# Residual of one row tile through TensorE, its normalise read from PSUM, its rows sent by halves of columns

## The chip, the cores and the metric

The kernel runs on one core of a Trainium2 chip. The metric is the device time of one execution in microseconds (us); the median of several runs is quoted, with its lowest and highest. A profile records one execution; its clock starts at the first instruction, and its span is about 1.8 us shorter than the device time.

## The reference, cut to what matters

```
def _layernorm(x): return (x - mean(x)) / sqrt(var(x) + 1e-5)      # over the 1024 columns

x = A_x                                     # 1 x 2048 x 1024, bf16
x = x + A(_layernorm(x), A_w_r, A_w_i)      # 2-D real FFT, times a complex filter, inverse FFT
x = x + B(_layernorm(x), w1, b1, w2)        # MLP: 1024 -> 3584, mish (the activation), 3584 -> 1024
x = x + A(_layernorm(x), ...)               # the second spectral layer
x = x + B(_layernorm(x), ...)
```

The change touches the seam between the second and the third of these lines: the end of the first MLP, and the layer norm and data movement that open the second spectral layer.

## The kernel before

The 2048 rows lie in SBUF, the working memory on the chip, as 16 tiles of 128 rows (`XS[:, j, :]`, bf16). PSUM is the memory that takes the matmul results, here as fp32 in banks of 512 columns. TensorE makes the second product of the MLP per row tile `j` and column half `h`, 28 matmuls into one PSUM bank. VectorE then adds that bank to the rows and takes statistics:

```
def mm2(c, t, h):
    j = 4 * c + t
    ...
    self.group(fns, reads=ra + r_w2, writes=[self.r_bank[bank]])        # 28 matmuls
    xs = self.XS[:, j, h * 512:(h + 1) * 512]
    self.op(dve, lambda e: e.tensor_tensor(xs, PS[:, bank, :], xs, ALU.add),
            reads=[self.r_bank[bank]], writes=[self.r_xs[j]])
    if not last:
        self.stats_half(j, h)                                          # bn_stats of 512 columns
    if h == 0:
        return
    ...
            self.root(j, 1)             # j >= 14: sqrt on ScalarE, reciprocal on VectorE
        b = self.apply(j, out=True)     # (x - mean) * r, 128 x 1024, SBUF to SBUF
        if j == 15:
            self.xr_direct(j, b)
        else:
            self.xn_store(j, b)         # the other tiles go by way of HBM
```

Dependences are kept in records: `self.r_xs[j]` is one record for the whole 1024-column row tile. An operation that reads a record waits for its last writer. `group` puts all waits of a group ahead of its first matmul. The last tile's rows go straight from SBUF to the spectral layer's input, in 16 transfers of 16 KB dealt to three issuing engines in turn; the first spectral matmul needs the first eight (the upper 64 rows):

```
def xr_direct(self, j, b):
    for i in range(16):
        half, h = i // 8, i % 8
        n = slice(64 * half, 64 * half + 64)
        prog = (self.sp, self.act, self.pool)[i % 3]
        self.dma(prog, self.XR.ap[row_of(j, h):row_of(j, h) + 1, n, :], b.ap[n, h * P:(h + 1) * P], ...,
                 reads=[b.res], parts=[self.r_xr[2 * half]])
```

After the MLP, 24 filler matmuls (`spin`) keep TensorE busy until the data arrives.

## Time and profile before

| | before |
|---|---|
| device time, median of 3 (lowest to highest) | 1017.54 us (1015.78 to 1019.77) |
| profiled span, granted clock | 1016.2 us, 0.998 |
| start of the last tile's first-half add, to first spectral matmul ("the seam") | 514.70 to 527.71, 13.01 us |
| of that, from the last MLP matmul to the first spectral one | 6.99 us |

I measure the seam from the first-half add because its start is set by work ahead of the edit (the first-half matmuls), so the seam holds the whole effect of the edit and nothing else. Its chain is shown in the prediction below. Beside it stand two lines of TensorE's timeline of the kernel before (start us, us, engine, line, operation, count, and in brackets the idle ahead with what ended it):

```profile
520.54 5.34 PE L628 MATMUL PS<-FD,BD 128*128 128x512 bf16 x24
527.71 6.85 PE L611 MATMUL PS<-M,ARENA 128*128 128x128 bf16 x104 [1.83 <-DMA ARENA<-ARENA]
```

The filler covers 5.34 us, then TensorE idles 1.83 us until the transfers have landed. So from the last MLP matmul on TensorE is not what the seam waits for. Ahead of that point it is: a matmul added there costs its own 0.22 us, little beside the add of 0.72 us that falls away, if it can start at once.

### The profile page before, as it was taken

How to read it: one execution, taken by the hardware profiler on the slowest of the kernel's cores; microseconds unless marked ns; L12 is line 12 of the kernel's file. 1: busy time of each engine (PE TensorE's matmuls, PEld its weight loads, DVE VectorE, ACT ScalarE, POOL GpSimd, SP SyncE). 2: the span in 40 equal slices, each digit the busy share in tenths (PEclk: the TensorE clock that was granted, in tenths of full speed). 3: DMA queues.
4: the chain of work that ended last, by engine and by line, in shares of the span. 5: the costliest groups of instructions: out<-in, count | busy, mean ns of one | idle time of the engine just before them, and what ended most of it. 6: DMA issues, size and time to landing. Idle time of an engine off the chain costs nothing.

```text
span 1016.2 us, 13732 instructions
## 1 busy us (share of the span) xinstructions
PE 955.1 (94%) x5779; PEld 507.3 (50%) x5865; DVE 326.5 (32%) x679; ACT 347.3 (34%) x482; POOL 81.5 (8%) x114
## 2 busy tenths in 40 slices
PE   0799799999999999999999978999999999999998
PEld 0577575444444444444456757644444444444443
DVE  6797469002444000033347736830011100000111
ACT  7798384330000433300029847543100024330000
POOL 4651000000000000002511100000000000000000
PEclk9999999999999999999999999999999999999999
DMA  9979813562111220002932875246411212100000
GB/s 283 247 221 320 212 61 114 181 205 72 47 46 32 73 83 21 1 21 82 195 66 82 233 188 140 89 156 207 126 27 46 73 52 80 45 1 11 21 26 27
DMA packets 154205, 107.00 MB, mean 105 GB/s; under 512 B 74448, under 2 KB 133664, under 8 KB 154144
## 3 DMA queue, kind: packets, MB, share of 16 engines
q1 hardware_dynamic: 143056, 78.61, 27.3%
q0 software_dynamic: 8912, 25.84, 8.8%
q10 hardware_dynamic: 2176, 1.66, 0.5%
q8 instruction: 47, 0.77, 0.3%
q14 instruction: 14, 0.11, 0.0%
HBM read 80.85 MB, written 20.71 MB: 100 GB/s over the span
## 4 chain that ended last, share of the span: by engine, by line
PE 86%; DVE 4%; DMA 4%; ACT 4%; issue 1%; SPq 0%; POOL 0%; ACTq 0%; DVEq 0%; POOLq 0%
PE PS L1057 38%; PE PS L1040 37%; PE PS L771 2%; PE PS L697 2%; PE PS L792 2%; DMA ARENA<-c_bt 1%; PE PS L950 1%; ACT ARENA L441 1%; DMA ARENA<-u_scratch 1%; DVE ARENA L619 1%; DMA XS<-in_A_x_dram 1%; ACT ARENA L550 1%; PE PS L1006 1%; DVE ARENA L592 1%; PE PS L810 1%
## 5 line engine op out<-in xcount | busy, mean ns | idle before, releaser
L1040 PE MATMUL PS<-ARENA 128*128 128x512 bf16 (+1 forms) x1950 | 389.3, 358 | 2.5 <-DVE ARENA L1011 0.6
L1057 PE MATMUL PS<-ARENA 128*128 128x512 bf16 x1756 | 385.5, 379 | 1.9
L1044 ACT ACTIVATE ARENA<-PS,B 128x512 bf16<-128x512 f32 (+1 forms) x248 | 158.9, 645 | 410.9 <-PE PS L1040 410.6
L1040 PEld LDWEIGHTS PS<-ARENA 128*128 128x128 bf16 x1984 | 192.8, 98 | 193.8 <-DVE ARENA L1011 1.5
L1057 PEld LDWEIGHTS PS<-ARENA 128*128 128x128 bf16 x1792 | 175.4, 98 | 211.4
L1062 DVE TENSOR_TENSOR XS<-PS,XS 128x512 bf16<-128x512 f32 x64 | 44.2, 691 | 587.1 <-PE PS L1057 587.1
L460 DVE BATCH_NORM_STATS2 BN<-XS 128x6 f32<-128x512 bf16 x100 | 64.7, 675 | 6.2 <-DMA XS<-in_A_x_dram 5.0
L550 ACT ACTIVATE ARENA<-PS 128x1440 bf16<-128x1440 f32 (+3 forms) x26 | 28.0, 1095 | 28.0 <-DVE XS L972 24.4
L249 POOL DMA_DIRECT2D xn_scratch<-ARENA x12 | 6.5, 541 | 374.5 <-DVE ARENA L512 374.5
L771 PE MATMUL PS<-ARENA 128*128 128x256 bf16 x256 | 32.4, 273 | 4.1 <-DVE ARENA L760 3.2
L778 ACT ACTIVATE ARENA<-PS 128x1024 bf16<-128x1024 f32 x32 | 33.0, 1051 | 7.1 <-PE PS L771 7.1
L432 ACT ACTIVATE RS<-MV,EPS 128x2 f32<-128x2 f32 (+2 forms) x5 | 1.5, 298 | 96.8 <-DVE MV L463 96.2
L697 PE MATMUL PS<-FD,ARENA 128*128 128x256 bf16 (+1 forms) x256 | 31.8, 271 | 2.4 <-ACT ARENA L617 1.2
L749 ACT ACTIVATE ARENA<-PS 128x1024 bf16<-128x1024 f32 x32 | 32.5, 1044 | 4.5 <-PE PS L745 4.5
L771 PEld LDWEIGHTS PS<-ARENA 128*128 128x128 bf16 x256 | 24.2, 98 | 11.8 <-DVE ARENA L760 5.5
L753 DVE TENSOR_TENSOR ARENA<-ARENA 128x1024 bf16<-128x1024 bf16 x32 | 22.0, 688 | 20.4 <-ACT ARENA L749 20.3
L697 PEld LDWEIGHTS PS<-FD,ARENA 128*128 128x128 bf16 x256 | 24.4, 98 | 6.5 <-DVE ARENA L619 1.4
L820 ACT ACTIVATE ARENA<-PS 128x1024 bf16<-128x1024 f32 x26 | 26.7, 1063 | 2.4 <-PE PS L792 2.4
L792 PE MATMUL PS<-ARENA,BD 128*128 128x256 bf16 x192 | 24.9, 273 | 2.3 <-ACT ARENA L778 2.3
L950 PE MATMUL PS<-MT,ARENA 128*128 128x32 bf16 (+1 forms) x512 | 20.9, 195 | 4.5 <-DMA ARENA<-u_scratch 2.5
L512 DVE TENSOR_SCALAR ARENA<-XS,MV,RS 128x1024 bf16<-128x1024 bf16 x48 | 24.8, 542 | 1.0
L732 ACT ACTIVATE ARENA<-PS 128x1024 bf16<-128x1024 f32 x22 | 22.9, 1058 | 3.1 <-PE PS L697 3.1
(76 smaller groups left out, 515.5 us busy)
## 6 DMA issues: line engine op xcount, KB each, us to landing
ARENA<-in_B_w_dram SPq DMA_DIRECT2D x56, 512.0 KB, 3.9
ARENA<-in_B_w_dram SPq DMA_DIRECT2D x56, 256.0 KB, 4.1
u_scratch<-ARENA SPq DMA_DIRECT2D x14, 512.0 KB, 3.7
ARENA<-u_scratch SPq DMA_DIRECT2D x14, 512.0 KB, 6.1
w_scratch<-ARENA POOLq DMA_DIRECT2D x8, 512.0 KB, 6.2
ARENA<-w_scratch POOLq DMA_DIRECT2D x8, 512.0 KB, 5.4
out_dram<-XS SPq DMA_DIRECT2D x16, 256.0 KB, 2.0
ARENA<-xn_scratch POOLq DMA_DIRECT2D x15, 256.0 KB, 10.0
```

The source lines that it names most:

```text
L460: self.op(self.dve, lambda e: e.bn_stats(self.BN[:, j, 6 * h:6 * h + 6], self.XS[:, j, 512 * h:512 * h + 512]), reads=[self.r_xs[j]], part ...
L550: fn = (lambda e: e.activation(dst, src, ACT.Copy)) if scale is None else \
L697: fns.append(lambda e: e.matmul(dst, at(r), FD[:, t:t + n], start=start, stop=stop))
L749: self.op(act, lambda e: e.activation(x.ap.rearrange("p a b -> p (a b)"), ps, ACT.Copy, scale=SIG), reads=banks, writes=[x.res])
L771: fns.append(lambda e, c=c, part=part: e.matmul(ps[:, c * 256:(c + 1) * 256], yk.ap[:, part, c * P:(c + 1) * P], t[:, (128, 0)[part]:(384, ...
L778: self.op(act, lambda e: e.activation(v.ap[:, :, i, :], src, ACT.Copy), reads=banks, parts=[v.res])
L792: fns.append(lambda e, dst=dst, part=part, c=c: e.matmul(dst, BD[:, c:c + P], mov(kd, part), start=(part == 0), stop=(part == 1)))
L950: fns.append(lambda e, l=l: e.matmul(self.PS[:, bank + l // k, l % k * w:(l % k + 1) * w], self.UT.ap[:, u0 + l, :], self.MT[:, 8 * lo:8 * ...
L1040: fns.append(lambda e, db=db, bank=bank, fl=fl: e.matmul(PS[:, bank, 0:w], wb.ap[:, db, fl * P:(fl + 1) * P], x.ap[:, db, tok], start=(db ...
L1044: self.op(act, lambda e, bank=bank, ft=ft: e.activation(at.ap[:, ft, tok], PS[:, bank, 0:w], ACT.Mish, bias=self.B1[:, ft:ft + 1]), reads= ...
L1057: fns.append(lambda e, i=i, ft=ft: e.matmul(PS[:, bank, :], at.ap[:, ft, t * P:(t + 1) * P], W2[ft].ap[:, h * 512:(h + 1) * 512], start=(i ...
L1062: self.op(dve, lambda e: e.tensor_tensor(xs, PS[:, bank, :], xs, ALU.add), reads=[self.r_bank[bank]], writes=[self.r_xs[j]])
```

## The change

The intent is to shorten the serial chain at the seam. For the last tile's right half, the residual becomes an identity matmul at the head of the accumulation group, so the add on VectorE falls away. Statistics and normalise read PSUM directly. The normalise is split by columns, so that the left half of the rows leaves early. ScalarE writes the finished right half back to `XS` afterwards. The core of the diff:

```
-    def xr_direct(self, j, b):
-        b.unread = False
-        for i in range(16):
+    def xr_direct(self, j, b, rows):
+        for i in rows:
 ...
+    def finish_last(self, bank):
+        j, dve, ps = 15, self.dve, self.PS[:, bank, :]
+        rb, r = self.r_bank[bank], self.r_mv[15]
+        self.op(dve, lambda e: e.bn_stats(self.BN[:, j, 6:12], ps), reads=[rb], parts=[r])
+        self.op(dve, lambda e: e.bn_aggr(self.MV[:, j, :], self.BN[:, j, :]), reads=[r], writes=[r])
+        self.root(j, 1)
+        b = self.xn_out[0]
 ...
+        for h in range(2):
+            src = ps if h else self.XS[:, j, 0:512]
+            self.op(dve, lambda e, h=h, src=src: e.tensor_scalar(b.ap[:, 512 * h:512 * h + 512], src, mean, rs, ...),
+                    reads=[rb if h else self.r_xs[j], r, self.r_rs[j]], parts=[b.res])
+            self.xr_direct(j, b, range(4, 16) if h else range(4))
+        self.copy(self.act, self.XS[:, j, 512:1024], ps, [], [rb, self.r_xs[j]])
 ...   in mm2:
+            summed = not last and (j, h) == (15, 1)
+            if summed:
+                fns.append(lambda e: e.matmul(PS[:, bank, :], self.IDENT[:], self.XS[:, j, 512:1024], start=True, stop=False))
 ...
-            self.group(fns, reads=ra + r_w2, writes=[self.r_bank[bank]])
+            self.group(fns, reads=ra + r_w2 + ([self.r_xs[j], self.r_ident] if summed else []), writes=[self.r_bank[bank]])
+            if summed:
+                self.finish_last(bank)
+                return
```

More of the change, by code (lines that the diff above doesn't have):

```diff
@@ L541, in xr_direct @@
                      reads=[b.res], parts=[self.r_xr[2 * half]])
+    def finish_last(self, bank):
[5 more added lines that the diff above has]
+        b = self.xn_out[0]
+        assert not b.unread
+        mean, rs = self.MV[:, j, 0:1], self.RS[:, 2, j:j + 1]
+        b.res.begin()
+        for h in range(2):
+            src = ps if h else self.XS[:, j, 0:512]
+            self.op(dve, lambda e, h=h, src=src: e.tensor_scalar(b.ap[:, 512 * h:512 * h + 512], src, mean, rs, op0=ALU.subtract, op1=ALU.mult),
+                    reads=[rb if h else self.r_xs[j], r, self.r_rs[j]], parts=[b.res])
+            self.xr_direct(j, b, range(4, 16) if h else range(4))
+        self.copy(self.act, self.XS[:, j, 512:1024], ps, [], [rb, self.r_xs[j]])
     def pair(self):
@@ L1058, in mm2 @@
                     PS[:, bank, :], at.ap[:, ft, t * P:(t + 1) * P], W2[ft].ap[:, h * 512:(h + 1) * 512],
-                    start=(i == 0), stop=(i == NF - 1)))
-            self.group(fns, reads=ra + r_w2, writes=[self.r_bank[bank]])
+                    start=(i == 0 and not summed), stop=(i == NF - 1)))
+            self.group(fns, reads=ra + r_w2 + ([self.r_xs[j], self.r_ident] if summed else []), writes=[self.r_bank[bank]])
+            if summed:
+                self.finish_last(bank)
+                return
             xs = self.XS[:, j, h * 512:(h + 1) * 512]
@@ L1074, in mm2 @@
                     self.root(j, 1)
-                b = self.apply(j, out=True)
-                if j == 15:
-                    self.xr_direct(j, b)
-                else:
-                    self.xn_store(j, b)
+                self.xn_store(j, self.apply(j, out=True))
         w2v = self.w2.rearrange("(ft fp) d -> fp ft d", fp=P)
```

## The prediction

> **What bounds the kernel now.** I read the page first, for its shares and for the chain that ended last.
>
> ```profile
> span 1016.2 us, 13732 instructions
> PE 955.1 (94%) x5779; PEld 507.3 (50%) x5865; DVE 326.5 (32%) x679; ACT 347.3 (34%) x482; POOL 81.5 (8%) x114
> PE 86%; DVE 4%; DMA 4%; ACT 4%; issue 1%; SPq 0%; POOL 0%; ACTq 0%; DVEq 0%; POOLq 0%
> ```
>
> TensorE carries 86% of the chain, nearly all of it the two groups of MLP matmuls, which the change leaves alone but for one added matmul. Everything else that is edited runs once, at the seam between the first MLP and the second spectral layer, for the last of 16 row tiles. So the second view is the chain of waits restricted to that seam (columns: start us, us, what).
>
> ```profile
> 517.74 2.98 PE PS L1057 x13
> 520.72 0.03 issue
> ...
> 520.81 0.70 DVE XS L1062
> 521.52 0.02 issue
> 521.54 0.71 DVE BN L460
> 522.25 0.02 issue
> 522.27 0.22 DVE MV L463
> 522.49 0.03 issue
> 522.51 0.30 ACT RS L432
> 522.81 0.02 issue
> 522.84 0.17 DVE RS L434
> 523.01 0.03 issue
> 523.04 0.56 DVE ARENA L512
> 523.60 0.02 issue
> 523.62 0.57 ACTq L249
> 524.19 0.03 issue
> 524.22 0.86 ACTq L249
> 525.09 0.03 issue
> 525.12 2.25 DMA ARENA<-ARENA
> 527.37 0.35 issue
> 527.71 0.62 PE PS L611 x8
> ```
>
> The reader is to see a strictly serial stretch of 6.99 us, from the last MLP matmul (520.72) to the first spectral matmul (527.71): add of the residual, statistics, aggregate, root, reciprocal, normalise, then two transfer issues on ScalarE's queue ahead of a third that takes 2.25 us to land. That third is transfer 7 of 16 (ScalarE issues 1, 4, 7, ...); the first spectral group waits for transfers 0 to 7, the upper 64 rows. TensorE meanwhile runs 24 filler matmuls. The whole 6.99 us is 0.69% of the span: even if it vanished, the 2% line would not be crossed.
>
> The third view is the timeline of VectorE ahead of the seam, since the new matmul reads what VectorE writes there.
>
> ```profile
> 514.70 0.69 DVE L1062 TENSOR_TENSOR XS<-PS,XS 128x512 bf16<-128x512 f32 x1 [3.21 <-PE PS L1057]
> 515.43 0.69 DVE L460 BATCH_NORM_STATS2 BN<-XS 128x6 f32<-128x512 bf16 x1
> ```
>
> The first-half add starts only after the first-half matmuls are complete (514.70), and TensorE meanwhile goes straight on with the second half. I will need that below.
>
> **What the Trainium skill says.** "VectorE: DVE Perf Modes", section "The perf-mode tier table (the rule you actually need)": a tensor_scalar on bf16 in SBUF may run at 4x, any PSUM operand is capped lower, and its next section gives 1x for fp32 in PSUM. The trace agrees as far as it goes: the 128x1024 bf16 normalise took 547 ns, but a 128x1024 cast out of fp32 PSUM took 1214 ns. "TensorE: Matmul & The Clock Gate", "Back-to-back issue gap": about N/2.4+2.5 ns, 216 ns for 512 columns; here 36 matmuls in 7.77 us, 216 ns each. Same page, "Single matmul latency": (398+N)/2.4 ns, 379 ns, and the filler records do say 379 ns; so a restarted stream pays 379-216 = 163 ns once. "DMA: Bandwidth & Descriptors", "Anatomy of one DMA": about 2 us fixed whatever the size; the 16 KB pieces land 2.0 to 2.5 us after issue, so making work ready earlier can save only the issue ahead of that, not the landing.
>
> **The change part by part.** Times are on the clock of the profile above.
>
> (1) Residual through TensorE. The add of 0.70+0.02 = 0.72 us leaves the path. In comes an identity matmul of 216 ns at the head of the second-half group. It is not free to start at once: it reads the last tile's rows, and the kernel keeps one dependence record for the whole 1024-column tile, whose last writer is the first-half add. So TensorE, in order, must stop until 514.70+0.69 = 515.39, say 515.45 with semaphore and weight load. Without the change the second-half group starts at about 520.70-0.38-27x0.216 = 514.49. The stall is 515.45-514.49 = 0.96 us. The columns it needs (512 to 1023) were long ready, so the wait is false, but it is real time. The group now ends at 515.45+28x0.216+0.379 = 521.88 against 520.70: **+1.18 us**. The net of this part is +1.18-0.72 = +0.46 us.
>
> (2) Statistics from PSUM. The instruction still processes 512 elements, and the case's other PSUM-reading instruction of that length takes 691 ns against 695 for the SBUF form. I count **0**. Aggregate, root and reciprocal are unchanged: VectorE's second statistics begin at about 521.94, the reciprocal is done 1.49 us later (the stretch 521.52 to 523.01 before), at 523.43.
>
> (3) Normalise in two. The SBUF half (512 bf16) I estimate at 0.35 to 0.41 us: 547 ns for 1024, with the fixed part between 154 ns (a 128x1 tensor_scalar in this trace) and 280 ns (what is left of 547 if it streams at 4x). The PSUM half at 1x I estimate at 0.69 to 0.78. They need no wait between them, and such pairs overlap by about 0.09 us (two full ones took 1.00, not 1.09). Together 1.0 to 1.1 us against 0.55: first half done at 523.85, second at 524.55, against 523.59 before. **+0.96 us** for the last data, of which +0.50 comes from this part.
>
> (4) Transfers. Numbers 0 to 3 (left columns of the upper rows) go out at 523.87, while the second normalise runs. When the right half is ready, ScalarE has only 4 and 7 left of what gates the spectral layer, one issue (0.60 to 0.90 us) ahead of the decisive one, not two (523.62 to 525.12 = 1.50 us). Number 7 therefore starts at 524.57+0.60..0.90 = 525.17..525.47, against 525.12, and lands 2.25 us later, 527.4 to 527.7. SyncE's number 6 follows its number 3 at about 525.1 and lands with 2.3 us at 527.4; GpSimd's 5 is earlier. So this part gives back 0.6 to 0.9, I take **-0.74 us**.
>
> (5) Writing back the right half of the rows. ScalarE copies it out of PSUM, 597 ns for such a copy in this trace, after its last issue: done near 528.0. It frees its PSUM bank for the second spectral group, which I count (pairs go round four; the first group uses banks 2 and 3, the second 4 and 5, the MLP's last result is bank 4) and which would start near 528.5. Off the path, with half a microsecond to spare.
>
> Sum: +0.46 (1, 2) +0.50 (3) -0.74 (4) = **+0.22 us**. The gap from last MLP matmul to first spectral matmul shrinks from 6.99 to about 6.05 us, but the matmul group before it grows by 1.18. What is delayed at the seam is passed on: after it TensorE, ScalarE's evictions and the transposed transfers again form one chain.
>
> **The rivals.** (A) The intended reading: residual matmul hidden, nothing stalls. Then TensorE grows only 0.22 us and the seam ends about 0.75 us earlier: near 1016.8. For it: the input columns really are ready. Against: the record is by tile, and the program waits on it. (B) The ScalarE copy ends late, holds bank 4 and delays the second spectral group by up to 0.5 us; also ScalarE's first eviction (528.80 before) queues behind it: near 1018.2. For it: ScalarE's issue of 0.86 us shows that the queue can hiccup. Against: the spare half microsecond. (C) Clock: TensorE now pauses 0.96 us inside the MLP and about 0.9 us after the filler. The skill's TensorE page, "What's actually happening", ties throttling to an idle window of some 3.4 us; here a pause of 1.83 us before the spectral layer already left the granted clock at 1.00, so I expect none. If it did drop, the spectral stage's first microseconds would run at half speed: +2 to 4 us, still under 2%.
>
> **Range and chances.** The median before is 1017.54, and its three runs span 1015.78 to 1019.77, eighteen times my net effect. Predicted: 1017.54+0.22, so 1017.7 us. The range is set by that run-to-run spread for a median of few runs, about 2 us each way: 1015.7 to 1019.7. No mechanism here can reach 20 us, so within 2% has 0.99.
>
> **What would show each step.** In the changed profile: an idle of 0.8 to 1.1 us on TensorE inside the last MLP group, ended by VectorE's write of the rows (step 1; if it is absent, A holds); no add, and a PSUM statistics of about 0.7 us (2); two normalise instructions of about 0.4 and 0.7 us (3); four transfers issued before the rest and one issue, not two, ahead of the deciding one (4); a ScalarE copy of 0.6 us that nobody waits for (5; if TensorE's second spectral group waits for it, B holds). A granted clock under 1.00 after the seam would mean C. I am wrong on the whole if the seam, counted from the first-half add to the first spectral matmul (13.0 us before), moves by more than 0.6 us either way.

## The result, and the profile after

| | before | after |
|---|---|---|
| first comparison, 4 runs each | 1016.79 us (1015.78 to 1019.77) | 1019.5 us (1019.28 to 1020.71) |
| ratio after/before, 95% interval | | 1.0024 (1.0001 to 1.0048) |
| second comparison | 1017.61 us, 11 runs | 1018.33 us, 6 runs |
| ratio, 95% interval | | 1.0002 (0.9985 to 1.0019) |
| profiled span | 1016.2 us | 1017.5 us |
| seam | 13.01 us | 13.26 us (second profile 13.30) |

Ratios here are the mean time of one kernel's fast runs over that of the other's of the same rounds, so they are not quite the ratio of the medians. The result is far within 2%.

The chain of waits of the changed kernel through the seam (start us, us, what; line numbers have moved: L1087 is the first-half add, L1077 the identity matmul, L547 the statistics from PSUM, L556 the two normalises, L629 the first spectral matmuls):

```profile
515.93 0.70 DVE XS L1087
...
516.68 0.39 PE PS L1077
...
523.14 0.71 DVE BN L547
...
524.65 1.14 DVE ARENA L556 x2
...
525.82 0.75 ACTq L249
...
526.59 2.25 DMA ARENA<-ARENA
...
529.19 0.62 PE PS L629 x8
```

Where the old chain of the second half began with TensorE, this one begins with VectorE's first-half add: TensorE waits for it. The second-half add is gone, and only one issue on ScalarE's queue is left ahead of the deciding transfer (before: two). The seam is 529.19-515.93 = 13.26 us. The chain saved 0.92 us after the MLP's matmuls (from 6.99 us to 529.19-523.12 = 6.07) and lost 1.17 us ahead of their end (from 520.72-514.70 = 6.02 us to 523.12-515.93 = 7.19), so it lost more than it saved. TensorE's own timeline of the changed kernel shows the loss as idle time:

```profile
516.68 0.39 PE L1077 MATMUL PS<-XS,IDENT 128*128 128x512 bf16 x1 [0.79 <-DVE XS L1087]
522.95 5.34 PE L646 MATMUL PS<-FD,BD 128*128 128x512 bf16 x24
529.19 6.85 PE L629 MATMUL PS<-M,ARENA 128*128 128x128 bf16 x104 [0.90 <-DMA ARENA<-ARENA]
```

Idle ahead of the spectral layer fell from 1.83 to 0.90 us, but 0.79 us of new idle stands inside the MLP, ended by VectorE's write of `XS`. And VectorE's and ScalarE's timelines of the changed kernel:

```profile
524.65 0.41 DVE L556 TENSOR_SCALAR ARENA<-XS,MV,RS 128x512 bf16<-128x512 bf16 x1
524.98 0.80 DVE L556 TENSOR_SCALAR ARENA<-PS,MV,RS 128x512 bf16<-128x512 f32 x1
528.58 0.60 ACT L568 ACTIVATE XS<-PS 128x512 bf16<-128x512 f32 x1 [4.16 <-issue]
```

The half that reads PSUM takes twice as long as the half that reads SBUF. ScalarE's copy ends at 529.18; the second spectral group, which needs that bank, would start at 529.19+0.62 = 529.81.

**Where the rest of the 1.3 us of span went.** The first-half add itself stood 1.23 us later in the changed kernel's profile (515.93 against 514.70), ahead of anything edited. So I split all 14 profiles at fixed instructions:

| stretch | over all 14 profiles, us |
|---|---|
| start to the first column transform of spectral layer 1 | 38.8 to 41.1 |
| from there to the first matmul after its scratch round trip through HBM | 74.0 to 77.1 |
| from there to the first mish of the MLP (layer 1; layer 2) | 13.56 to 14.13; 13.56 to 14.29 |
| first MLP, from its first to its last mish (second MLP the same) | 296.22 to 296.23 |
| from there to the first-half add | 89.96 |
| the seam | 12.29 to 14.06 |
| first spectral matmul to the next stage (one experiment apart) | 9.91 |
| from there to the first matmul after the second scratch round trip | 68.9 to 69.9 |

The MLP repeats to 0.01 us. Most of the scatter lies in the spectral layers, in and after the stretches that load from HBM and go through it: in the first spectral layer the unchanged kernel alone took 74.75, 76.00 and 75.27 us in three profiles, the changed one 76.55 and 77.11. A seam can therefore be compared to 0.05 us, and a whole time only to one or two.

The traces also hold what goes with this scatter: the granted clock of TensorE. In 11 of the 14 profiles it falls to half for 3.41 us, once or twice, somewhere in the spectral layers. From the first column transform to the first mish of layer 1, the seven profiles without such a stretch took 87.57 to 88.85 us (mean 88.09), the seven with one or two took 88.61 to 90.67 (mean 89.75). The changed kernel's profile has one at 105.47 us, the profile of the kernel before has none in that layer (its only one is at 608.77), and this is where the 1.23 us arose: 90.11 us against 88.85. Over 45 timed runs of the kernel before, the 8 with a mean clock of 0.999 or more averaged 1017.1 us, the 22 with 0.997 or less 1019.6. This is a correlation: no experiment here sets the clock.

### The profile page after: what moved, and what is told of

Same layout as the page of the kernel before. It is cut to its first block, busy times and chain, and to the rows that moved or that the text cites. A ratio compares the mean times of both kernels' runs of the same rounds, so it can differ in the third digit from the quotient of the medians.

```text
span 1017.5 us, 13734 instructions
## 1 busy us (share of the span) xinstructions
PE 956.8 (94%) x5780; PEld 507.8 (50%) x5866; DVE 327.8 (32%) x679; ACT 347.9 (34%) x483; POOL 81.5 (8%) x114
## 4 chain that ended last, share of the span: by engine, by line
PE 86%; DMA 4%; DVE 3%; SPq 3%; ACT 3%; issue 1%; POOL 0%; ACTq 0%; DVEq 0%; POOLq 0%
PE PS L1079 38%; PE PS L1058 37%; SPq L249 3%; PE PS L789 2%; PE PS L715 2%; PE PS L810 2%; DMA ARENA<-in_A_w_i_dram 1%; PE PS L968 1%; DMA ARENA<-c_bt 1%; DMA ARENA<-u_scratch 1%; ACT ARENA L568 1%; PE PS L828 1%; PE PS L1024 1%; PE PS L761 1%; ACT ARENA L796 1%
## 5 line engine op out<-in xcount | busy, mean ns | idle before, releaser
L1087 DVE TENSOR_TENSOR XS<-PS,XS 128x512 bf16<-128x512 f32 x63 | 43.6, 692 | 581.3 <-PE PS L1079 581.3
```

## The experiments

All outputs are right. Each seam is read from the run's profile. "Before" is 13.01 us and "after" 13.26 us.

**1. The kernel before against itself (label same), five rounds.** No edit.

> The kernel before, unchanged, against itself. Theory 1 (only the seam moved, +0.25 us; the rest of the measured difference of 0.24% is scatter between runs): seam from the first-half add to the first spectral matmul 13.0 us as before, and a ratio that can be off 1.000 by 0.1 to 0.2% although nothing differs. Rival (the changed kernel really loses some 2.4 us, most of it outside the seam): this run gives 1.000 within 0.1%, and its first-half add starts near 514.7 us, as in the first profile.

Measured: seam 13.04 us; 1019.14 us against 1017.61 us, ratio 1.001 (0.9992 to 1.0027). Identical programs differed by 1.5 us in the median. The bare first ratio of 1.0024 is not much beyond that. The slower set was also granted less clock, 0.9958 on average against 0.9974. Its profile has the first-half add at 515.45 us, ahead of any edit 0.75 later than in the first profile.

**2. The changed kernel again (label after_again), five rounds.** No edit.

> The changed kernel again. Theory 1: seam 13.26 us, ratio 1.000 to 1.001 (the seam's +0.25 us is 1.0002). Rival: ratio about 1.0024 again, and the first-half add again more than 1 us later than in the kernel before's profiles of the same call.

Measured: seam 13.30 us, ratio 1.0002 (0.9985 to 1.0019). The seam repeated, the 0.24% did not. The first-half add of this profile came at 517.12 us, 1.67 later than in the profile of label same. That is the rival's second sign, and it came true; its first, a ratio of 1.0024, did not. The lateness arose ahead of the edit: spectral layer 1 took 77.11 us to the first matmul after its round trip, with two half-clock stretches (105.59 and 119.24 us) against one (115.70) in label same.

**3. The wait on the first-half add taken away (label nostall), five rounds.** The identity matmul gets a record for the right half of the columns alone, copied before the first-half add writes the left half:

```
+            if (j, h) == (15, 0):
+                self.r_right = Res('XS15r')
+                self.r_right.inherit(self.r_xs[j])
-            self.group(fns, reads=ra + r_w2 + ([self.r_xs[j], self.r_ident] if summed else []), ...)
+            self.group(fns, reads=ra + r_w2 + ([self.r_right, self.r_ident] if summed else []), ...)
```

> The changed kernel with a dependence record of its own for the right half of the last tile, so that the identity matmul does not wait for the first-half add. If the stall is what eats the gain: no idle of TensorE inside the last MLP group, which ends 0.96 us earlier, and the seam falls from 13.26 to 12.3 us, 0.7 us better than before; ratio near 0.9993 to 1.000. If the stall was hidden by later waits (filler, transfers), the seam stays at 13.2 to 13.3 us.

Measured: seam 12.38 us. TensorE's timeline and the chain of this kernel:

```profile
515.61 0.38 PE L1077 MATMUL PS<-XS,IDENT 128*128 128x512 bf16 x1
```

```profile
525.52 2.32 DMA ARENA<-ARENA
...
528.19 0.62 PE PS L629 x8
```

No idle stands ahead of the identity matmul, which starts 0.20 us before the first-half add (515.81). The filler starts 6.06 us after that add instead of 7.02, 0.96 us earlier as expected; the seam gains 0.88, since the deciding transfer took 2.32 us and not 2.25. So the stall turned a gain of 0.63 us (13.01 to 12.38) into a loss of 0.25. The whole time can't show it: 1018.14 us, ratio 1.0 (0.9985 to 1.0014).

**4. Nothing but the false wait, on the kernel before (label stallonly), one look.**

```
-            self.group(fns, reads=ra + r_w2, writes=[self.r_bank[bank]])
+            self.group(fns, reads=ra + r_w2 + ([self.r_xs[j]] if not last and (j, h) == (15, 1) else []), ...)
```

> The kernel before plus nothing but the false wait: the second-half matmuls of the last tile wait for the first-half add. Accounting: TensorE idles 0.8 us, restart costs another 0.16, seam 13.0+0.96 = 13.97 us. If a pause there is absorbed by later waits, the seam stays 13.0 us.

Measured: seam 14.06 us, 1.05 more than before (expected 0.96). In TensorE's timeline:

```profile
514.56 6.22 PE L1057 MATMUL PS<-ARENA 128*128 128x512 bf16 x27 [0.79 <-DVE XS L1062]
```

The same 0.79 us of idle, with no other part of the change in the kernel. The filler starts 6.80 us after the first-half add against 5.84 before, so the wait costs 0.96 us, as in experiment 3 (the idle and the restart of the stream); the other 0.09 us is the deciding transfer, which took 2.34 us and not 2.25. The cost of the wait is shown from both sides.

**5. The identity matmul last instead of first (label identlast), one look.**

```
-                fns.append(lambda e: e.matmul(PS[:, bank, :], self.IDENT[:], self.XS[:, j, 512:1024], start=True, stop=False))
 ...   after the 28 matmuls:
+            if summed:
+                fns.append(lambda e: e.matmul(PS[:, bank, :], self.IDENT[:], self.XS[:, j, 512:1024], start=False, stop=True))
```

> The changed kernel with the identity matmul as the last of its group in place of the first; but the group's waits stand ahead of its first matmul in this program, so the wait on the first-half add is still taken before matmul 1. If the wait (and not the place of the identity matmul) costs the time, this shows the same stall and a seam of 13.26 us. If the place matters, 12.3 us.

Measured: seam 13.31 us. The timeline of TensorE shows the wait ahead of matmul 1 and the identity matmul at the end:

```profile
516.62 6.22 PE L1079 MATMUL PS<-ARENA 128*128 128x512 bf16 x27 [0.79 <-DVE XS L1089]
522.67 0.38 PE L1083 MATMUL PS<-XS,IDENT 128*128 128x512 bf16 x1
```

The place of the matmul is nothing; where the program puts the wait is all. Had `group` placed each wait at the matmul that needs it, this version would probably not have stalled; that was not tried.

**6. All 16 transfers after the right half (label late), one look.**

```
-            self.xr_direct(j, b, range(4, 16) if h else range(4))
+        self.xr_direct(j, b, range(16))
```

> The changed kernel with all 16 transfers issued after the right half is ready, none early. Accounting: ScalarE has two issues ahead of the deciding one again, 0.6 to 0.9 us more: seam 13.26+0.75 = 14.0 us. Rival (the early transfers buy nothing): 13.26 us.

Measured: seam 14.00 us, 0.74 more than the changed kernel. The four early transfers are worth what the prediction took for them.

**7. Only the split (label split), five rounds, three times.** The kernel before, with the right-half add kept on VectorE and both halves normalised out of SBUF:

```
+                    for c in range(2):
+                        cs = slice(512 * c, 512 * c + 512)
+                        self.op(dve, lambda e, cs=cs: e.tensor_scalar(b.ap[:, cs], self.XS[:, j, cs], mean, rs, ...), ...)
+                        self.xr_direct(j, b, range(4, 16) if c else range(4))
```

> The kernel before with only the normalise and its transfers split by halves of columns; the residual stays on VectorE and everything is read from SBUF. My accounting: the two normalises of about 0.41 us overlap a little, the right half is ready 0.2 us later than before, one issue on ScalarE's queue drops out of the path, so the deciding transfer starts 0.15 to 0.4 us earlier: seam 12.6 to 12.85 us against 13.0. Rival: the issue queue, busy from the first four transfers, sets the pace and nothing is gained, seam 13.0 us.

Measured: seam 12.91 us, between the expectation (12.85 at most) and the rival (13.0), so the expected gain was missed; ratio 0.9977 (0.9961 to 0.9993). The chain of this kernel shows why the seam gains only 0.1 us:

```profile
523.32 0.75 DVE ARENA L1081 x2
524.07 0.27 ACTq L249
...
524.37 0.86 ACTq L249
```

The right half is ready at 524.07, but ScalarE's queue is still issuing its early transfer until 524.34, and the issue after that takes 0.86 us. Here the queue sets the pace, as the rival said; in the changed kernel the slow PSUM half hides it.

The ratio did not fit a 0.1 us gain, so the same kernel ran again, once beside other kernels and once beside the kernel before:

> The split-only kernel once more. Its first five rounds gave 0.9977 (0.9961 to 0.9993) while its seam was only 0.1 us shorter (12.91 us). If the rest was scatter of the spectral layers' scratch round trips: seam 12.9 us again, and a ratio between 0.998 and 1.002 that need not repeat 0.9977. If it is a real gain of 2 us outside the seam: 0.9977 again within 0.001.

Measured: seam 12.94 us, ratio 0.9983 (0.9968 to 0.9998).

> Split only, a third time (0.9977 and 0.9983 so far, seams 12.91 and 12.94 us). If the 2 us are scatter: nearer 1.000 this time, between 0.999 and 1.001. If they are a real effect outside the seam: 0.997 to 0.9985 a third time, with a seam of 12.9 us all the same. I now hold the second for as likely as the first.

Measured: seam 12.95 us, ratio 0.9993 (0.9979 to 1.0008). And the kernel before against itself (label same_again):

> The kernel before against itself a second time; the first time gave 1.001 (0.9992 to 1.0027) with medians 1.5 us apart. If two loads of one program on one chip can differ by a microsecond or two in most of their runs, this ratio is off 1.000 by 0.001 to 0.002 in one direction or the other, with a seam of 13.0 us. If not, it is within 0.0005 of 1.000.

Measured: seam 13.02 us, ratio 1.0009 (0.9991 to 1.0026), again above 1. A comparison of two identical programs was thus off by 0.1% both times. Whether the split kernel wins a microsecond or so outside its seam stays open: its three ratios all lie below 1 and shrink towards it, and the seam accounts for 0.1 us. The clock could account for most of the rest: its 18 runs were granted 0.9987 on average, the 45 of the kernel before 0.9972, and that difference is worth at most 0.0015 x 1017 = 1.5 us (an estimate), where the means differ by 1.65 us. Whether that was luck or the split's doing is not shown.

**8. No stall, and the transfers dealt anew (label best), five rounds.** On top of experiment 3. The text below says that no queue then has two issues left after the right half; that is not so. Transfers 4 to 7 all need the right half, and three queues share them: the new deal moves the pair from ScalarE's queue (4 and 7) to SyncE's (4 and 7), whose first issue is shorter.

```
-            prog = (self.sp, self.act, self.pool)[i % 3]
+            prog = dict(S=self.sp, A=self.act, P=self.pool)['SAPPSAPSASPASPAS'[i]]
```

> The no-stall kernel with the transfers dealt to the queues anew: of the eight that gate the spectral layer, SyncE issues 0, 4, 7, ScalarE 1 and 5, GpSimd 2, 3, 6, so that no queue has two issues left after the right half. Accounting from the no-stall trace: the last of the eight is issued about 0.15 us earlier and on a queue that lands it sooner, so it lands 0.3 to 0.4 us earlier: seam 12.0 us against 12.38 (no stall) and 13.0 (before). Rival (the landing time of about 2.3 us grows when queues are dealt otherwise): 12.3 us or more. The whole time can't resolve this: ratio 0.999 with scatter of 0.002.

Measured: seam 12.29 us, against an expected 12.0; 1017.49 us against 1018.65 us, ratio 0.9992 (0.9979 to 1.0005), so not resolved in the whole time. In the chain of this kernel SyncE's third issue decides, with one issue of 0.49 us ahead of it where experiment 3 had 0.75 us on ScalarE's queue:

```profile
523.52 0.49 SPq L249
...
524.05 2.37 DMA ARENA<-ARENA
526.42 0.46 issue
```

It landed 11.82 us after the first-half add, 0.22 earlier than the deciding transfer of experiment 3 (527.85-515.81 = 12.04). Half of that was given back between landing and first matmul (0.46 against 0.35 us). TensorE waits there for three queues' semaphores one after another, and a different one comes last; that this is the 0.1 us is argued, not shown. Its seam lies at the edge of what its rival gave (12.3 us or more). It is the shortest of all, 0.7 us under before, which is 0.07% of the span.

**9. The copy out of PSUM four times (label copy4), one look.** In the changed kernel:

```
-        self.copy(self.act, self.XS[:, j, 512:1024], ps, [], [rb, self.r_xs[j]])
+        for _ in range(4):
+            self.copy(self.act, self.XS[:, j, 512:1024], ps, [], [rb, self.r_xs[j]])
```

> The changed kernel with ScalarE's copy out of PSUM made four times over instead of once (same result). If the copy is 0.6 us short of mattering, as the traces of the changed kernel say: three more copies end about 1.3 us after the second spectral group would have started, that group waits for them, and the stretch from the first spectral matmul to the next stage grows from 9.91 to 11.1 to 11.4 us; the seam itself stays 13.3 us. If the copy already delayed things, the stretch grows by the full 1.9 us.

Measured: seam 13.27 us, and the stretch from the first spectral matmul to the next stage 12.66 us, 2.75 more than 9.91 and well past both expectations. The group did wait for the copies, 1.31 us. The rest shows in the windows (stretch: us, busy us and count by engine, then the granted clock, DMA share, GB/s):

```profile
528.06 6.87 PE L630 MATMUL PS<-M,ARENA 128*128 128x128 bf16 x88 [1.31 <-ACT XS L569]
```

```profile
528.00:530.00 2.00, 1.94 (x22) 1.95 (x23) 0.32 (x2) 1.02 (x2) 0.00 (x0) 0.60 0.00 0
530.00:532.00 2.00, 2.00 (x23) 2.00 (x22) 1.52 (x2) 1.02 (x1) 0.00 (x0) 0.54 0.00 0
```

The granted clock fell to 0.60 and 0.54 in these two windows; in the record it is half from 528.42 us for 3.41 us. TensorE had idled 0.91 us for the transfers, worked 0.61, then idled 1.31. In the changed kernel the clock over the same stretch was 1.00. So a single copy costs nothing, as predicted, but beyond its margin the cost was more than a plain wait: 2.75-1.31 = 1.44 us came on top while the clock was low. This is the only one of the 14 profiles with a half-clock stretch at the seam. That the second pause so soon after the first brought it about is likely, but argued from one execution.

## Why the prediction was right

The prediction gave 1017.7 us in 1015.7 to 1019.7; the two sets gave 1019.5 and 1018.33 us. It holds, near the top of the range. That hit says little: the range of 4 us is eighteen times the effect, and came from the scatter. What tests the mechanism is the seam and its steps, each counted from the first-half add:

| step | predicted, us | measured, us |
|---|---|---|
| (1) identity matmul starts | +0.75 | +0.75 |
| (1) matmul group ends | +7.18 | +7.19 |
| (2) statistics from PSUM | 0.69 | 0.70 |
| (2) reciprocal done | +8.73 | +8.70 |
| (3) left half, right half | 0.35 to 0.41, 0.69 to 0.78 | 0.41, 0.80 |
| (3) right half ready | +9.85 | +9.86 |
| (4) deciding transfer issued | +10.47 to 10.77 | +10.66 |
| (4) worth of the early transfers | -0.74 | -0.74 (experiment 6) |
| (5) ScalarE's copy, spare before it matters | 0.60, about 0.5 | 0.60, 0.63 |
| sum: seam against before | +0.22 | +0.25; +0.26 (second profile, against 13.04 in label same) |

**Step 1** was the step that mattered, and it is shown three ways: the idle in the changed profile, its return when it alone is added (experiment 4), and its going when the record is split (experiment 3). **Step 3** was slightly under-sized for the PSUM half, 0.80 against at most 0.78. With its own upper value for the fixed part, 280 ns, the prediction would have had 0.81. That the right half was ready as predicted is luck: the reciprocal came 0.03 us early. **Step 4** was right in its mechanism; that the point taken from 0.6 to 0.9 us was met to 0.01 is luck too. One reading was loose: the two MLP groups carry 75 of the chain's 86%, which is not nearly all. **Rival A** described what the kernel would have been without the false wait, and its size of 0.75 us was nearly that of experiment 3 (0.63). **Rival B** did not occur; experiment 9 shows that it would take more than the one copy. **Rival C** did not occur at the seam: the clock stayed at 1.00 until 610.64 us, and the drop there has its like in the kernel before (608.77). But "I expect none" rested on the single pause of 1.83 us, and in experiment 9 the clock fell after two shorter pauses in close succession. That reason was weaker than the text made it, while the cost it named, 2 to 4 us, was above the 1.44 us of experiment 9.

What the prediction had no term for is the remaining offset of the first set of runs, 0.24%. It did not repeat, the scatter it would have to exceed is shown in experiment 1, and the stretch in which the profile has it lies ahead of the edit and holds a half-clock stretch. I therefore put it down to scatter, not to the change; that is argued, not shown. Against it stand the first interval, which leaves out 1, and the runs at an equal clock of 0.998: six of the changed kernel average 1018.9 us, 15 of the kernel before 1017.5.

## What to carry to other kernels

When an operation moves to another engine, look at what its inputs' dependence record covers: here one record for 1024 columns made TensorE stop 0.79 us for 512 columns that it did not read, and the 0.96 us that this cost was more than the 0.63 us that the rest of the change saved. A serial seam is measured best between two fixed instructions around the edit, since it repeats to 0.05 us where the whole time scatters by 2 us or more. And before work is cut out ahead of transfers, count the issues per queue: splitting the data early helps only as far as the queue is free when the second part is ready.

## What the Trainium skill lacked or had wrong

- "TensorE: Matmul & The Clock Gate", section "Why this matters for your kernels", advises no idle gap over about 3 us. No gap reached that here, and the clock still fell to half: in experiment 9 for 3.41 us after pauses of 0.91 and 1.31 us with 0.61 us of work between, and in the spectral layers of 11 of the 14 profiles, where TensorE's longest pause was 2.07 us. One pause of 1.83 us at the seam of the kernel before left it at 1.00. So a limit on single gaps is not enough. The page's section "A second HAM failure mode: psum-queue depth-cycling" does tell of frequent micro-idles, but gives no length; these runs show none either, since executions of one kernel differ in whether and where the clock falls.
- "VectorE: DVE Perf Modes", section "The TRN2 errata — SBUF-src ops pay a fixed extra latency per instruction", gives VectorE one fixed cost per source memory in its table, and about 150 cycles as measured. Here tensor_scalar with mean and scale taken from SBUF took 547 ns for 1024 bf16 columns, 411 ns for 512, and 803 ns for 512 fp32 columns from PSUM. At 4x, 4x and 1x of 0.96 GHz that leaves 280, 278 and 270 ns of fixed cost (4x and 1x by the tier table and its subsection on PSUM operands, which the prediction cites; an estimate), where the tensor_tensor from PSUM (692 ns) leaves 159 and bn_stats from PSUM (700 ns) 167. A 128x1 tensor_scalar with constants took 154 ns in all. The page has no such extra for operands of this kind; that the operands are its cause is argued from this comparison.
- "DMA: Bandwidth & Descriptors", section "Issuing engines are not separate DMA queues", calls the issue time that several issuing engines save usually small beside the transfer. At this seam it decided: 0.49 to 0.87 us per issue against 2.0 to 2.6 us to land one of the deciding 16 KB pieces, and 0.74 us for the issues taken off the path (experiment 6).
